# A fused retention and channel-mix kernel: a new hand order of all pieces, one block moved to full chunks, two scalings moved off GpSimd, and the last tile cut in three

## The chip, the core and the metric

The kernel runs on one core of a Trainium2 chip. The time is in device microseconds (us) of that core; a figure for a kernel is the median of its runs. The core has five engines that run side by side, each through its own list of instructions in order: TensorE (PE in the profile; its weight loads are PEld), VectorE (DVE), ScalarE (ACT), GpSimd (POOL) and SyncE (SP). An engine waits at an instruction until the semaphores that it names have been raised, and everything behind that instruction on the same engine waits too. Transfers between device memory and the on-chip memory (SBUF) are put in queues by SP, ACT and POOL. TensorE writes its products to PSUM, eight banks of 128 x 512 float32.

## The reference

The first part is a retention recurrence per head. The second is a channel mix with a shift by one token:

```python
# B=4, H=8, S=768, D=64; gamma[h] = 1 - 2**(-5-h); scale = 1/8
for t in range(S):
    state = gamma * state + outer(k[t], v[t])     # 64 x 64 per batch and head
    y[t] = scale * q[t] @ state
x = y, heads side by side                         # B x 768 x 512
xk = mu_k * x + (1 - mu_k) * x_prev               # x_prev: x one token earlier
xr = mu_r * x + (1 - mu_r) * x_prev
k = relu(xk @ w_k)                                # 512 -> 1024
v = (k * k) @ w_v                                 # 1024 -> 512
out = sigmoid(xr @ w_r) * v
```

Inputs and output are float32. The kernel computes the products in float16 with float32 sums, and turns the recurrence into products over chunks of tokens.

## The kernel before, in words

The 4 x 768 tokens are 12 **blocks** n = 0..11 of 256 tokens, three to a batch. All work is cut into **pieces**, and one text, `ORDER` (lines 24 to 75), lists them. The loop at line 745 reads it word by word and issues each piece. Since every engine runs its own pieces in this order, the text is the schedule; there is no other planner in the kernel. A word is a code, its arguments, after `~` an engine (v VectorE, a ScalarE, p GpSimd, s SyncE) and after `@` the PSUM banks. Counting an engine's words off along the timeline of the trace gives each instruction its piece, and the prediction names instructions so.

The pieces of a block n, with their engine and line:

- `lq`, `lk`, `lv`: loads of q, k and v (lines 232 and 237), nearly all from GpSimd's queue; a float32 source is written as float16 for q and k. v stays float32 and is multiplied by powers of gamma and cast in `vs` (line 255), on VectorE, for blocks 1 and 3 on GpSimd. `cq`, `ck` (line 245) are casts of the first half of block 0, which SP loads.
- `Tq`, `Tk`: TensorE transposes q and k (lines 274, 280); `Eq`, `Ek`: ScalarE copies them out of PSUM (line 243).
- `S`: scores k times q within a chunk (lines 320, 333, 341); `M`: VectorE copies them out under a causal mask (lines 349, 356).
- `C`: the block's part of the state, k times vs (lines 368, 386, 397); `U`: adds it to the carried state (line 421; for a batch's first chunk a copy, line 245 or 243); `G`: decays the state for the next block (line 426 on ScalarE, four instructions; the same function has a one-instruction form for VectorE).
- `I`, `J`: the product of q with the carried state (line 443); `Y`: masked scores times vs (lines 464, 480, 491). Both sum in one PSUM pair. `D`: VectorE scales it into x (lines 509, 516).
- `dx`: x minus x one token earlier (line 531). `X.n.w.j`: the mix for xk (w=0) or xr (w=1), columns j of four (line 560). Blocks 3 and 4, 6 and 7, 9 and 10 are mixed together (`GROUPS`).
- `K.n.g`: xk times w_k (lines 574, 584), after all four `X.n.0.j`; `Qa`, `Qb`: ScalarE's relu and square (lines 593, 601, 605). `R.n.tb`: xr times w_r (line 614), after all four `X.n.1.j`; `s`: sigmoid (line 620). `V.n.tb.half`: times w_v (line 626); `O`: VectorE's final product (line 632); `st`: the store (line 639).
- `z.c`: products of zeros on TensorE that nothing reads, c//4 of float32 and c%4 of float16 (lines 693, 700). `mu`, `mt`, `me`: load, transpose and copy of mu_k and mu_r (lines 676, 681, 684). `gy.0`, `gy.1`: a table of powers of gamma (lines 718, 711). `wk`, `wr`, `wv`: loads of the weights, on GpSimd's queue.
- `Vc`, `Oc`, `sc`: V, O and store of the very last 128 tokens by column parts (lines 644, 651, 659).

A block in `HALF` is worked in chunks of 64 tokens: 32 products of 64 x 64 for S, one mask instruction of 128 x 1024, three or four U, two instructions for D. A block in `WIDE` has chunks of 128 tokens: S in two parts with a mask instruction of 128 x 1024 each, one or two U, one D, and 16 products of 128 columns for Y. Before, blocks 2 to 4 are WIDE and 5 to 11 HALF.

```python
    def decayed(e, n):                       # G
        if e is nc.scalar:
            for j in range(NJ):
                nc.scalar.activation(...)
            return
        e.tensor_tensor(out=TG[0](n + 1), in0=T32(n), in1=gd[...], op=ALU.mult)
```

## Time and profile before

| | us |
|---|---|
| median of 3 runs (156.02 to 158.55) | 156.29 |
| the profiled execution | 156.68 |
| its span, first to last instruction | 154.9 |
| what lies around the span | 1.78 |
| TensorE busy | 146.0 |
| VectorE busy | 126.9 |
| ScalarE busy | 99.4 |
| GpSimd busy | 55.5 |
| bytes moved | 22.31 MB |

A record of a matmul holds its way through the array, so records overlap: four products of 512 columns are recorded with 379 ns each, but start 216 ns apart. What a piece costs TensorE is read from start to start. VectorE's records overlap by some 0.08 us when an instruction does not need the one before it, and stand 0.03 us apart when it does. The granted TensorE clock is 1.000 over the whole span.

### The profile page before, as it was taken

How to read it: one execution, taken by the hardware profiler on the slowest of the kernel's cores; microseconds unless marked ns; L12 is line 12 of the kernel's file. 1: busy time of each engine (PE TensorE's matmuls, PEld its weight loads, DVE VectorE, ACT ScalarE, POOL GpSimd, SP SyncE). 2: the span in 40 equal slices, each digit the busy share in tenths (PEclk: the TensorE clock that was granted, in tenths of full speed). 3: DMA queues.
4: the chain of work that ended last, by engine and by line, in shares of the span. 5: the costliest groups of instructions: out<-in, count | busy, mean ns of one | idle time of the engine just before them, and what ended most of it. 6: DMA issues, size and time to landing. Idle time of an engine off the chain costs nothing.

```text
span 154.9 us, 5520 instructions
## 1 busy us (share of the span) xinstructions
PE 146.0 (94%) x2423; PEld 83.9 (54%) x2423; DVE 126.9 (82%) x205; ACT 99.4 (64%) x186; POOL 55.5 (36%) x65
## 2 busy tenths in 40 slices
...
DMA packets 45768, 22.31 MB, mean 144 GB/s; under 512 B 37416, under 2 KB 41392, under 8 KB 45744
## 3 DMA queue, kind: packets, MB, share of 16 engines
...
q14 instruction: 5, 0.04, 0.1%
...
## 4 chain that ended last, share of the span: by engine, by line
PE 55%; DVE 24%; DMA 12%; issue 4%; POOL 3%; DVEq 0%; POOLq 0%
PE ps L626 19%; DMA v<-in_v_dram 12%; PE ps L614 9%; PE ps L574 9%; PE ps L584 8%; DVE a L356 3%; DVE xk L560 3%; DVE xr L560 3%; DVE vs L255 3%; DVE dx L531 2%; DVE xT L516 2%; DVE tg L421 2%; DVE os L632 2%; PE ps L443 2%; DVE a L349 1%
## 5 line engine op out<-in xcount | busy, mean ns | idle before, releaser
L626 PE MATMUL ps<-wv,k2s 128*128 128x512 f16 x184 | 43.4, 379 | 0.0
L593 ACT ACTIVATE kr<-ps 128x512 f32<-128x512 f32 x48 | 27.8, 596 | 23.1 <-PE ps L574 18.0
L626 PEld LDWEIGHTS <-k2s 128*128 128x128 f16 x184 | 17.4, 98 | 20.0
L632 DVE SCALAR_TENSOR_TENSOR os<-ps,rs 128x512 f32<-128x512 f32 x23 | 15.4, 683 | 14.5 <-ACT rs L620 7.4
L614 PE MATMUL ps<-wr,xr 128*128 128x512 f16 x96 | 24.1, 380 | 0.0
L584 PE MATMUL ps<-xk,wk 128*128 128x256 f16 x192 | 24.0, 273 | 0.0
L232 POOL DMA_DIRECT2D k<-in_k_dram x20 | 17.7, 898 | 15.2 <-PE ps L280 10.5
L574 PE MATMUL ps<-xk,wk 128*128 128x512 f16 x96 | 22.5, 379 | 0.0
L584 PEld LDWEIGHTS <-wk 128*128 128x128 f16 x192 | 18.1, 98 | 4.9 <-DMA wk<-in_moe_w_k_dram 0.6
L620 ACT ACTIVATE rs<-ps 128x512 f32<-128x512 f32 x24 | 13.7, 594 | 9.3 <-PE ps L614 8.9
L560 DVE SCALAR_TENSOR_TENSOR xr<-dx,mu,xT 128x256 f16<-128x256 f32 (+1 forms) x36 | 19.2, 564 | 0.1
L560 DVE SCALAR_TENSOR_TENSOR xk<-dx,mu,xT 128x256 f16<-128x256 f32 (+1 forms) x36 | 18.8, 567 | 0.2
L232 POOL DMA_DIRECT2D v<-in_v_dram x18 | 16.2, 915 | 1.4 <-DMA q<-in_q_dram 0.5
L243 ACT COPY kT<-ps 128x1024 f16<-128x1024 f16 (+1 forms) x13 | 12.2, 947 | 5.2 <-PE ps L280 4.1
L601 ACT ACTIVATE k2s<-kr 128x512 f16<-128x512 f32 x24 | 14.9, 628 | 0.3
L574 PEld LDWEIGHTS <-wk 128*128 128x128 f16 x96 | 9.2, 98 | 10.8
L531 DVE TENSOR_TENSOR dx<-xT 128x1024 f32<-128x1024 f32 x12 | 14.6, 1223 | 0.3
L605 ACT ACTIVATE k2s<-kr 128x512 f16<-128x512 f32 x24 | 14.5, 628 | 0.1
L243 ACT COPY qT<-ps 128x1024 f16<-128x1024 f16 (+1 forms) x13 | 12.3, 949 | 2.4 <-PE ps L274 2.2
L614 PEld LDWEIGHTS <-xr 128*128 128x128 f16 x96 | 8.8, 97 | 9.2 <-DVE xr L560 0.2
L255 DVE TENSOR_TENSOR vs<-v,csm_sb 128x1024 f16<-128x1024 f32 x10 | 12.1, 1216 | 2.0 <-DMA v<-in_v_dram 2.0
L356 DVE TENSOR_TENSOR a<-ps,c_sb 128x1024 f16<-128x1024 f32 (+1 forms) x12 | 12.2, 1040 | 0.5 <-PE ps L333 0.4
...
## 6 DMA issues: line engine op xcount, KB each, us to landing
...
wk<-in_moe_w_k_dram POOLq DMA_DIRECT2D x2, 512.0 KB, 11.0
...
```

The lines of the kernel that those rows point to most:

```text
L232: e.dma_start(out=dst[:, :, i * D : i * D + D], in_=src[:, i * P : i * P + P].rearrange("h p d -> p h d"),)
L243: e.copy(out=out, in_=in_)
L255: e.tensor_tensor(out=VS(n), in0=V32(n).rearrange("p h (i d) -> p i h d", i=2), in1=gks[:, int(half(n) or wide(n)), :, :, None].to_broadca ...
L356: nc.vector.tensor_tensor(out=a_full(n)[:, i, :, j0:j1], in0=pairs(banks("S", n, i, j0))[:, :, j0:j1], in1=(below if wide(n) else causal[: ...
L531: e.tensor_tensor(out=DX(k)[:, :, m * TM + t0 : m * TM + t1], in0=x[:, :, c + t0 : c + t1], in1=x[:, :, c - 1 + t0 : c - 1 + t1], op=ALU.s ...
L560: nc.vector.scalar_tensor_tensor(out=XM[w](k)[:, j, t0:t1], in0=DX(k)[:, j, t0:t1], scalar=mu[:, w * NCO + j : w * NCO + j + 1], in1=x[:, ...
L574: nc.tensor.matmul(banks("K", n, g), lhsT=wk16[:, co, g * P : g * P + P], rhs=XM[0](k)[:, co, :], start=(co == 0), stop=(co == NCO - 1),)
L584: nc.tensor.matmul(pz[:, i, :], lhsT=wk16[:, co, fo * P : fo * P + P], rhs=XM[0](k)[:, co, m * TM + t0 : m * TM + t1], start=(i == 0 and c ...
L593: nc.scalar.activation(out=kr, in_=banks("K", n, g, *u), func=AF.Relu)
L614: nc.tensor.matmul(banks("R", n, tb), lhsT=XM[1](k)[:, co, t : t + P], rhs=wr16[:, co, :], start=(co == 0), stop=(co == NCO - 1),)
L626: nc.tensor.matmul(banks("V", n, tb), lhsT=K2(n)[:, fo, tb * P : tb * P + P], rhs=wv16[:, fo, :], start=(fo == 0), stop=(fo == NFO - 1),)
L632: nc.vector.scalar_tensor_tensor(out=OS(2 * n + tb), in0=banks("V", n, tb), scalar=1.0 / (KSC * KSC), in1=RS(2 * n + tb), op0=ALU.mult, op ...
```

## The change

The words of `ORDER` are put in a new order. Beyond the order itself:

- Block 5 moves from HALF to WIDE: `S.5`, `M.5` become two parts each, `U.5.1` and `U.5.2` go, `J.5` comes.
- `vs.1` and `vs.3` move from GpSimd to VectorE. No computation is left on GpSimd, which then only queues transfers.
- `gy.1` moves from ScalarE to VectorE, `cq` from VectorE to ScalarE; `U.0.0`, `U.3.0` and `U.9.0` from VectorE to ScalarE; `G.7` and `G.9` from ScalarE to VectorE.
- The zero products are dealt out anew; the first word `z.12` becomes four words `z.3`. `mt` moves ahead of the first transposes.
- On the queues, `lk.0.0.2` now stands ahead of `lq.0.0.2` on SP, `lq.0.2.4` ahead of `lv.0` on GpSimd, `wk.1` behind `lv.2` and `lk.2`, both `wv` together; `lv.7` instead of `lv.11` is queued by SP.
- The last 128 tokens are cut into columns 0 to 255, 256 to 383 and 384 to 511 (`CUTS`) instead of two halves.

The diff, cut to the stretches that the prediction speaks of:

```diff
 KUP = 4.0
-HALF = (5, 6, 7, 8, 9, 10, 11)
+HALF = (6, 7, 8, 9, 10, 11)
...
-WIDE = (2, 3, 4)
+WIDE = (2, 3, 4, 5)
 HEADS = ((0, 1), (3, 2), (4, 5), (7, 6))
+CUTS = ((0, 256), (256, 384), (384, 512))
 ORDER = """
-lq.0.0.2~s gy.0 lv.0~p lk.0.0.2~s ck.0.0.2~v mu lk.0.2.4~p lq.0.2.4~p gy.1~a lv.1~p lk.1~p lq.1~p
-cq.0.0.2~v lq.2~p wk.0~p z.12@6 Tk.0.0.2@0 Tq.0.0.2@1 Ek.0.0.2~a Eq.0.0.2~a mt@2 wk.1~p vs.0~v
-z.2@6 S.0.0.0.2@01 me M.0.0.0.2~v S.0.1.0.2@45 Tk.0.2.4@2 M.0.1.0.2~v Tq.0.2.4@3 lk.2~p C.0@67
-U.0.0~v Ek.0.2.4~a Eq.0.2.4~a z.1@0 S.0.0.2.4@23 M.0.0.2.4~v I.0@45 S.0.1.2.4@01 M.0.1.2.4~v z.1@2
-Y.0 U.0.1 G.0~a vs.1~p Tk.1@7 Ek.1~a D.0~v dx.0~v lv.2~p lq.3~p lk.3~p C.1@01 U.1.0 X.0.0.0
-X.0.0.3 Tq.1@6 Eq.1~a z.4@2 S.1.1@67 lq.4~p X.0.0.2 I.1@45 Tq.2@0 M.1.1~v S.1.0@23 Eq.2~a wr~p
-X.0.0.1 z.1@7 K.0.0@6 M.1.0~v U.1.1 G.1~a lk.4~p Qa.0.0 X.0.1.0 X.0.1.1 Qb.0.0 Y.1 D.1~v dx.1~v
-X.1.0.1 z.1@3 K.0.3@7 X.1.0.2 Qa.0.3 K.0.2@1 X.1.0.0 Qa.0.2 X.1.0.3 Tk.2@6 K.0.1@0 Ek.2~a vs.2~v
-S.2.0@67 S.2.1@45 M.2.0~v Qb.0.3 K.1.1@1 K.1.2@2 Qa.0.1 Qb.0.2 lv.3~p C.2@0 Qa.1.2 Tq.3@3 Eq.3~a
-U.2.0 I.2@67 Tk.3@0 Qa.1.1 K.1.0@2 Tq.4@1 X.1.1.0 Ek.3~a Qa.1.0 M.2.1~v Y.2 lq.5~p Eq.4~a S.3.0@45
...
-R.1.1@7 X.2.0.1 vs.3~p M.3.0~v Ek.4~a K.2.3@1 Qa.2.3 K.2.0@6 Qa.2.0 M.3.1~v S.4.1@45 M.4.1~v
-Tq.5@1 Eq.5~a C.3@23 U.3.0~v U.3.1 s.1.1 vs.4~v R.1.0@6 s.1.0 G.3~a K.2.1@0 I.3@45 Qb.2.3 S.4.0@23
...
-lv.5~p vs.5~v K.3.5@0 Qa.3.5 Qa.3.3 K.3.4@6 V.1.1.1 Qa.3.2 lv.6~p C.5@01 S.5@45 Qa.3.4 vs.6~v
-C.6@23 Qb.3.3 Qb.3.2 O.1.1 M.5~v U.5.0 X.2.1.3 U.5.1 U.6.0~a U.6.1 U.6.2 U.5.2 U.6.3 K.3.0@6
...
-Qb.5.1 V.4.0.1 X.6.0.1 lq.9~p G.7~a V.3.0.0@3 V.3.1.1 V.3.0.1 U.8.0 K.6.3@4 Qa.6.3 O.4.0 K.6.1@5
...
-G.9~a vs.11~v U.10.0 U.10.1 U.10.2 Qb.6.5 M.10~v st.5.1 R.6.0@1 s.6.0 R.7.0@0 s.7.0 K.8.1@1 Qa.8.1
...
-Qb.11.1 X.11.1.1 O.8.0 K.11.3@1 s.9.1 V.9.1.0@3 V.10.1.0@0 s.8.1 O.8.1 st.8.1 R.11.1@6 V.9.0.0@7
-Qa.11.3 V.11.0.0@1 s.10.0 Qa.11.2 Qb.11.2 R.10.1@2 V.9.1.1 O.9.1 V.10.1.1 s.10.1 O.10.1 st.9.1
-Qb.11.3 V.9.0.1 st.10.1 s.11.1 Vc.11.1.1@2 s.9.0 V.10.0.0@6 O.9.0 R.11.0@0 V.11.0.1 st.8.0 st.9.0
-s.11.0 Oc.11.1.1 sc.11.1.1~a O.11.0 st.11.0 V.10.0.1 O.10.0 st.10.0 Vc.11.1.0@0 Oc.11.1.0
-sc.11.1.0~s
+lk.0.0.2~s lq.0.2.4~p lq.0.0.2~s lv.0~p mu z.3@6 z.3@6 z.3@6 z.3@6 mt@0 cq.0.0.2~a ck.0.0.2~v
+Tk.0.0.2@1 Ek.0.0.2~a Tq.0.0.2@2 Eq.0.0.2~a me z.4@6 S.0.0.0.2@23 gy.0 gy.1~v Tq.0.2.4@1
+Eq.0.2.4~a vs.0~v S.0.1.0.2@45 lk.0.2.4~p Tk.0.2.4@0 Ek.0.2.4~a C.0@67 M.0.0.0.2~v U.0.0~a
+M.0.1.0.2~v S.0.0.2.4@01 M.0.0.2.4~v lv.1~p I.0@23 S.0.1.2.4@45 U.0.1 M.0.1.2.4~v z.3@0 Y.0 vs.1~v
+G.0~a D.0~v dx.0~v X.0.0.1 X.0.0.0 lk.1~p Tk.1@4 Ek.1~a lq.1~p z.3@0 Tq.1@5 Eq.1~a z.4@3 S.1.1@45
+lq.2~p Tq.2@2 Eq.2~a C.1@67 X.0.0.3 X.0.0.2 U.1.0 z.2@3 I.1@01 M.1.1~v S.1.0@23 M.1.0~v wk.0~p
+K.0.1@6 Qa.0.1 K.0.0@4 Qa.0.0 X.0.1.3 U.1.1 lv.2~p vs.2~v Qb.0.1 Y.1 D.1~v dx.1~v lk.2~p z.5@2
+C.2@4 Tk.2@5 G.1~a U.2.0 z.1@2 I.2@01 wk.1~p K.0.3@4 X.1.0.3 Ek.2~a S.2.0@67 Qa.0.3 S.2.1@23
+Qb.0.3 X.1.0.1 X.1.0.0 X.1.0.2 K.1.1@5 K.0.2@4 Qa.1.1 Qb.1.1 lk.3~p K.1.0@5 X.0.1.2 Qa.0.2 X.0.1.0
...
+K.2.0@5 s.0.1 Qb.0.2 Qa.2.0 K.2.2@1 vs.3~v C.3@67 U.3.0~a Qa.2.2 M.3.0~v lk.5~p Tk.5@0 Ek.5~a
+S.4.0@45 lv.4~p S.4.1@23 U.3.1 I.3@67 G.3~a K.2.1@1 K.1.3@0 M.4.0~v vs.4~v Qa.2.1 Qb.2.1 Y.3
...
+D.3~v dx.3~v Y.4 K.2.3@5 S.5.0@67 M.5.0~v J.4 X.2.1.0 D.4~v dx.4~v s.1.1 wv.0~p Tk.6@01 Qa.2.3
...
+K.3.7@1 vs.5~v Qa.3.7 O.0.0 O.0.1 Qb.3.3 lv.6~p st.1.1 S.5.1@23 vs.6~v S.6@67 M.6~v Tq.7@45 Eq.7~a
+C.5@0 R.2.0@1 U.5.0 lv.7~s C.6@67 U.6.0~a I.5@45 K.3.2@0 s.2.0 Qa.3.2 Qb.3.2 M.5.1~v Y.5 U.6.1
+U.6.2 U.6.3 S.7@23 M.7~v I.6@01 J.5 K.3.6@6 vs.7~v G.6~a K.3.5@7 K.3.4@2 D.5~v dx.5~v X.5.0.1
...
+lq.10~p X.6.0.2 vs.8~v K.5.0@1 X.5.1.2 X.5.1.3 G.7~v Qa.5.0 Qb.5.0 lv.10~p V.4.0.1 O.3.0 st.2.0
...
+S.9@01 Tq.10@67 M.9~v Y.8 D.8~v dx.8~v X.8.0.2 X.8.0.3 V.5.1.0@4 K.6.4@0 G.9~v R.6.0@1 R.5.0@2
...
+O.9.1 V.10.0.0@3 st.9.1 s.10.0 Vc.11.1.1@5 V.10.1.1 R.11.1@6 O.9.0 s.10.1 O.10.1 st.9.0 V.11.0.0@7
+V.10.0.1 O.10.0 st.10.1 s.11.1 st.10.0 R.11.0@6 s.11.0 Oc.11.1.1 sc.11.1.1~a V.11.0.1 O.11.0
+Vc.11.1.0@2 st.11.0 Oc.11.1.0 sc.11.1.0~s Vc.11.1.2@6 Oc.11.1.2 sc.11.1.2~a
 """
...
     def values_c(e, n, tb, c):
-        x = slice(c * dm // 2, (c + 1) * dm // 2)
+        x = slice(*CUTS[c])
...
     def result_c(e, n, tb, c):
-        x = slice(c * dm // 2, (c + 1) * dm // 2)
+        x = slice(*CUTS[c])
...
     def store_c(e, n, tb, c):
-        x = slice(c * dm // 2, (c + 1) * dm // 2)
+        x = slice(*CUTS[c])
```

More of the change, by code (lines that the diff above doesn't have):

```diff
@@ new lines @@
+S.9@01 Tq.10@67 M.9~v Y.8 D.8~v dx.8~v X.8.0.2 X.8.0.3 V.5.1.0@4 K.6.4@0 G.9~v R.6.0@1 R.5.0@2
+X.8.0.1 Eq.10~a s.6.0 V.5.1.1 O.5.1 s.5.0 C.10@67 U.10.0 U.10.1 I.9@23 Qa.6.4 Qb.6.2 Tq.11@01
+Qb.6.4 Eq.11~a V.5.0.1 U.10.2 R.6.1@4 s.6.1 U.10.3 Qb.6.6 S.10@01 G.10~a I.10@67 Y.9 X.8.0.0
+M.10~v K.8.3@4 st.3.0 K.8.0@0 Qa.8.3 D.9~v Qa.8.0 R.7.1@1 vs.11~v s.7.1 K.8.2@4 C.11@23 Qa.8.2
+Qb.8.0 Qb.6.7 Tk.11@01 O.5.0 st.5.0 st.5.1 U.11.0 U.11.1 U.11.2 Y.10 D.10~v Ek.11~a V.7.0.0@5
+V.6.0.0@4 I.11@23 S.11@01 M.11~v X.8.1.1 X.8.1.2 dx.9~v dx.10~v X.9.0.0 X.9.0.3 X.9.0.2 V.7.0.1
```

54 lines of the change are left out of this document (25 added, 29 removed).

## The prediction

> **What bounds the kernel now.** I read the busy times first, then the chain of waits, then the groups by shape, then the timeline, whose instructions I named by counting off the words of ORDER. On the page:
>
> ```profile
> PE 146.0 (94%) x2423; PEld 83.9 (54%) x2423; DVE 126.9 (82%) x205; ACT 99.4 (64%) x186; POOL 55.5 (36%) x65
> ```
>
> Two engines are nearly full (its first part: busy time, share of the span), so the question is which one ends last where. The chain of waits in order of time (start, length, what) answers it:
>
> ```profile
> 8.16 0.45 DVE vs L255
> ...
> 74.64 0.43 DVE tg L421
> 75.08 0.04 issue
> 75.12 0.29 PE ps L443 x12
> ...
> 150.42 0.89 PE ps L644 x8
> 151.31 0.02 issue
> 151.33 0.42 DVE os L651
> ```
>
> Mostly VectorE sets the pace until 75 us; from then TensorE runs to 151.3 almost without a gap. Busy time in stretches of the span shows the same (the stretch, its length, then busy us and instructions of PE, PEld, DVE, ACT and POOL; granted clock, DMA share, GB/s):
>
> ```profile
> 16.00:20.00 4.00, 2.91 (x75) 2.21 (x79) 4.00 (x8) 1.01 (x1) 1.33 (x2) 1.00 1.56 191
> 130.00:140.00 10.00, 10.00 (x64) 6.06 (x63) 2.42 (x5) 9.03 (x18) 0.00 (x0) 1.00 0.07 26
> ```
>
> At 16 to 20 us VectorE is full and TensorE is not; at 130 to 140 it is the reverse. VectorE's last mix (X.11.1.1) ends at 131.03. So the end is: the time at which VectorE lets TensorE into its dense run, plus all TensorE work behind that point, plus what TensorE still waits. A change of order must be judged by this sum. I take it at K.1.1, the first point of dense running that both orders pass with almost the same pieces done. From the timeline (start, length, engine, what):
>
> ```profile
> 7.58 0.20 PE L681 MATMUL ps<-csm_sb,mu 8*128 8x8 f32 x1 [0.84 <-DMA mu<-in_moe_mu_r_dram]
> ...
> 24.23 0.62 PE L333 MATMUL ps<-qT,kT 64*128 64x128 f16 x16
> 24.79 1.95 PE L584 MATMUL ps<-xk,wk 128*128 128x256 f16 x16
> ...
> 38.92 0.44 PE L386 MATMUL ps<-vs,k 128*64 128x64 f16 x16 [0.52 <-POOL vs L255]
> ```
>
> The second line is S.2, the third begins with K.1.1: it starts at 24.79, and TensorE ends 151.29 - 24.79 = 126.5 later.
>
> **The change: VectorE's own work.** The groups by shape (count, busy time, mean ns of one, idle time before):
>
> ```profile
> L255 DVE TENSOR_TENSOR vs<-v,csm_sb 128x1024 f16<-128x1024 f32 x10 | 12.1, 1216 | 2.0 <-DMA v<-in_v_dram 2.0
> L255 POOL TENSOR_TENSOR vs<-v,csm_sb 128x1024 f16<-128x1024 f32 x2 | 3.8, 1918 | 3.7 <-DMA v<-in_v_dram 3.6
> L421 DVE TENSOR_TENSOR tg<-ps,tg 128x256 f16<-128x256 f32 x22 | 9.0, 417 | 0.4
> L356 DVE TENSOR_TENSOR a<-ps,c_sb 128x1024 f16<-128x1024 f32 x8 | 9.7, 1218 | 0.5 <-PE ps L333 0.4
> ```
>
> Two scalings come to VectorE: 2 x 1.22 = 2.43. G.7 and G.9 are not shown there; nearest is U at 0.42 (bounds 0.29 and 0.68, VectorE's rows of half and twice the size): 0.84. gy.1 (128 x 512) lies between 0.42 (128 x 256, L718) and 1.22: the 128 x 512 mask takes 0.68, I take 0.69. cq leaves: -0.41. Three first copies U leave: 3 x -0.42 = -1.25. Block 5 wide: two U less (-0.84), one mask more (+1.22), one D of 1.23 for two of 0.69 (-0.15): +0.23. A third Oc: +0.16, as two of 128 columns at about 0.29 (L718, 128 x 128) stand for one of 0.42. Sum: +2.7, so VectorE goes from 126.9 to 129.6.
>
> GpSimd's scalings might have cost VectorE more than they show. They ran at 10.97 to 12.91 and 36.97 to 38.88. VectorE's masks and U beside them took 0.69, 0.42 and 1.22, their usual times, so I give nothing back.
>
> **The start.** mt now stands ahead of the first transposes, and mu_r's transfer ended it at 7.58 in this profile; Tk, before at 6.11, comes at about 7.65. Ek and Eq (0.59 each) then end at 9.2, z.4 beside them costs two records at 0.53, and S of block 0 follows by 9.6. v now is second in GpSimd's queue, behind a half load of q. It landed at 8.14 before; the halves behind it landed 0.4 and 1.2 later, so I take 8.6. k, now first on SP, lands near 4.0 as q did, so ck, gy.0 (2.05) and gy.1 (0.69) run ahead, 4.0 to 7.5, in a wait. vs.0 starts at 8.65, not 8.16, and covers the late transposes; without that cover (mu later than 7.7) every 0.1 goes straight into the sum.
>
> From vs.0 VectorE now does, until the end of U.2.0, at start-to-start rates read from the timeline (vs 1.14, M 1.13 and 0.61 for a half, U 0.34, D 1.26, dx 1.25, X 0.40): 3 vs 3.42; 4 half M 2.44; 2 M 2.26; 4 U 1.36; 2 D 2.52; 2 dx 2.50; 5 X 2.00. Together 16.5. The second k half is queued third and lands at about 9.3, as the third did; its transpose, copy and scores end at 11.5 and hold up the third mask by 0.5. So U.2.0 ends at 25.7. TensorE stands there: I.2 (0.3) waits for U.2.0, and K.0.3 (0.87), S.2 (0.66) and K.1.1 are queued behind I.2. K.1.1 starts at 27.6: **2.8 later than before**. The new zero products (twelve at first, then z.3, z.3, z.4, z.2, z.5, z.1) all lie ahead of this point, beside VectorE's work, and cost nothing as long as that is longer.
>
> **Behind K.1.1.** Of the pieces done ahead of it, K.0.2 is now behind (+0.87), C.2 and I.2 are ahead (-0.45). Block 5 wide: S 0.66 as S.4 for 0.38 as S.6; C 0.15 for 0.19; I, J and Y 1.0 for 0.56 in all (as block 4 against block 5): +0.65. The last tile's two pieces of 128 columns replace one of 256, 8 x 0.109 = 0.87. A product of this form is not shown. It costs no less than the columns, half of 0.109, and no more than 0.109; the transposes of 128 columns (0.6 for 16, two side by side) put it near 0.065, so +0.2 (bounds 0 and 0.87). The Trainium skill, "TensorE: Matmul & The Clock Gate", section "Back-to-back issue gap", gives 81 ns for 128 columns with weight loads, which would make it +0.43; it gives 131 ns for 512 columns too, where this trace has 216, so I stay with the rows. Sum: 126.5 + 0.87 - 0.45 + 0.65 + 0.2 = 127.8.
>
> In these 126.5 TensorE waits some 2.0 in six gaps, by the starts: 0.49 before I.2, 0.68 before C.3, and four of 0.15 to 0.25. C.3's goes: it waited for GpSimd's vs.3, which began when v landed (36.83) and took 1.9. VectorE reaches vs.3 at about 38 and needs 1.22. I take 0.8 off. What is late next: VectorE's words from vs.0 to the last mask of block 5 sum to 52.6 at these rates, so with 0.6 of waits it is there at 61.9, and TensorE at Y.5 at 62.8. A margin of 0.9 is why I take off no more.
>
> **The sum.** TensorE ends at 27.6 + 127.8 - 0.8 = 154.6 (before 151.3). Before, 3.6 followed to the end of the span; a last Oc of 128 columns saves 0.1: 3.5. Span 158.1. With 1.78 around it: 159.9 against the profiled 156.68. The median lies 0.39 under that execution, so the median comes to 159.5.
>
> **Rivals.** *The front runs without the waits that I put in.* v lands no later than before, the third mask doesn't wait, VectorE starts at 8.16: K.1.1 at 26.6, and the gaps behind shrink to 1.2, as in the forecast. Then 158.5. For it: VectorE has work to fill a wait, such as vs.1 between Y.0 and D.0, where it stood 0.52. Against: its work up to U.2.0 is fixed.
>
> *The front slips further.* mt at the head of TensorE, or loads behind a changed queue. mu_r's last packet started at 6.72 behind packets of k and v; if it lands 1 us later, transposes, S and all masks follow. Or TensorE's waits stay 2.0 and bank reuse adds as much as before. Each alone gives 160.5 to 161; both 162.
>
> *Not slower: TensorE's pieces shrink.* Taken each at its shortest start-to-start time in this trace (K, R and V 0.86, S of a half block 0.27, Tq 0.26, C 0.19, Y 0.41), the pieces in the 126.5 come to 117. The 9.5 above that are the 2.0 of gaps and a stretch of pieces around a change of shape: a K of 0.87 takes 0.97 behind 64-column products, Tq 0.41. If the new order groups like pieces and finds every result ready, so that half of it goes (4.7), TensorE ends at 150.7 and the median is 155.6. It decides from 4 us upward, where the 2.8 of the front and the 1.3 of added work are paid. Against: TensorE can get only 0.9 ahead before it stands at VectorE, by the count at Y.5.
>
> *GpSimd's scalings held VectorE.* If VectorE stood for both (3.84), that time comes back and the median is 155.7. No VectorE instruction beside them is longer than usual, and its longest stand there (0.52 ahead of D.0) ends with TensorE. The Trainium skill, "SBUF — State Buffer", section "Who interferes with whom", says that a VectorE instruction with two SBUF inputs and a GpSimd instruction that reads SBUF shut each other out for the whole instruction. This trace has no such pair: every VectorE instruction beside the scalings had an input in PSUM.
>
> **Chances.** Forecast 0.52 (159 to 161); front without waits 0.25; front slips 0.19; pieces that shrink 0.03; scalings that held VectorE 0.01. A measurement of this kernel can tell about 2% from no change: 159.4 and 153.2 are the bounds. The forecast lies on the upper one; 0.38 of its 0.52 is above, with the slip 0.57. The rest up to 1 is within 2%, but for 0.02 faster. The range leaves out the last two and the far end of the slip: 157.4 to 161.8.
>
> **What would show it.** Right: K.1.1 at 27 to 28 us, TensorE waiting for U.2.0 just ahead; VectorE busy 129 to 130; no wait of C.3 for vs.3; TensorE's last product near 154.6. Wrong: K.1.1 at 25 or earlier, a TensorE run behind it shorter than 126, or VectorE idle for several us because TensorE or a load is late.

## The result and the profile after

The changed kernel takes **156.81 us** (median of 20 runs, 156.14 to 158.35), the kernel before 156.45 in the same comparison (20 runs, 155.58 to 159.44). The ratio is 1.0038, with a 95% interval from 1.002 to 1.0056: 0.2 to 0.6% slower, where 2% was forecast. A repetition gave 156.54 against 156.18 (ratio 1.0016, 0.9991 to 1.0042, which includes no change). The ratio leaves out the four executions of the kernel before that took 158.3 us and more, and "at full clock" below means the median of the executions with a mean granted clock of 0.995 or more (the last section shows what happens in others), set beside the same median of the kernel before in that run's comparison, 156.0 to 156.5. The changed kernel has 156.57 at full clock, and 156.54 in the repetition.

The profiled execution took 156.27 us, its span is 154.5. Its busy times, and then the shares by engine in the chain of waits, from the profile's page:

```profile
PE 147.5 (95%) x2381; PEld 84.6 (55%) x2381; DVE 129.5 (84%) x205; ACT 98.8 (64%) x178; POOL 51.8 (34%) x63
```

```profile
PE 84%; DVE 6%; DMA 4%; issue 3%; ACT 1%; POOL 1%; POOLq 0%; DVEq 0%
```

VectorE's work came out as forecast (129.6). But the chain now lies on TensorE for 84% of the span. The same line of the kernel before has 55% there, with 24% on VectorE and 12% on transfers:

```profile
PE 55%; DVE 24%; DMA 12%; issue 4%; POOL 3%; DVEq 0%; POOLq 0%
```

Busy time in stretches of the changed kernel (stretch, length, then busy us and instructions of PE, PEld, DVE, ACT, POOL; then the granted clock, the DMA share and GB/s):

```profile
16.00:20.00 4.00, 3.92 (x106) 2.87 (x97) 3.93 (x8) 1.61 (x2) 2.18 (x3) 1.00 1.61 214
26.44:151.08 124.64, 124.64 (x1988) 71.69 (x1984) 107.63 (x163) 85.75 (x154) 32.40 (x37) 1.00 0.79 132
130.00:140.00 10.00, 10.00 (x63) 5.98 (x62) 3.81 (x8) 7.33 (x15) 0.00 (x0) 1.00 0.27 99
```

The second row is the prediction's "behind K.1.1": TensorE is busy in all of its 124.64 us. The same row of the kernel before, from its K.1.1 to its last product, has 1.1 us of idle time between its records:

```profile
24.79:151.29 126.50, 125.39 (x2052) 71.24 (x2048) 107.61 (x165) 85.48 (x158) 36.06 (x40) 1.00 0.81 131
```

So the later entry (26.44 instead of 24.79) is given back by a run that is 1.9 us shorter, although work was added to it. The entry in the timeline of TensorE after: the stand for U.2.0, which the prediction named, and, behind K.0.3 and S.2, K.1.1 as the first piece of the last row:

```profile
24.67 0.31 PE L444 MATMUL ps<-qT,tg 64*64 64x128 f16 x8 [1.01 <-DVE tg L422]
...
26.44 2.79 PE L585 MATMUL ps<-xk,wk 128*128 128x256 f16 x24
```

The scalings, from the groups: twelve at the same 1.22 us, and the wait for v that was 2.0 us in all is 0.6.

```profile
L256 DVE TENSOR_TENSOR vs<-v,csm_sb 128x1024 f16<-128x1024 f32 x12 | 14.6, 1221 | 0.6 <-DMA v<-in_v_dram 0.6
```

By kind of piece, from start to start behind K.1.1, the time that went is: q's transposes 4.78 to 3.49 (the stands before I.2 and C.3 came behind Tq.3 and Tq.5, which took 0.94 and 1.16, now 0.54 and 0.47), C 2.95 to 2.55, I 1.99 to 1.62, S 4.02 to 3.76 with one more part. K grew by 0.31, with one more in the stretch, and V by 0.28.

### The profile page after: what moved, and what is told of

Its sections match the earlier page's. It is cut to its first block, busy times and chain, and to the rows that moved or that the text cites. A ratio compares the mean times of both kernels' runs of the same rounds, so it can differ in the third digit from the quotient of the medians.

```text
span 154.5 us, 5438 instructions
## 1 busy us (share of the span) xinstructions
PE 147.5 (95%) x2381; PEld 84.6 (55%) x2381; DVE 129.5 (84%) x205; ACT 98.8 (64%) x178; POOL 51.8 (34%) x63
## 4 chain that ended last, share of the span: by engine, by line
PE 84%; DVE 6%; DMA 4%; issue 3%; ACT 1%; POOL 1%; POOLq 0%; DVEq 0%
PE ps L627 26%; PE ps L615 14%; PE ps L575 14%; PE ps L585 13%; DMA v<-in_v_dram 4%; PE ps L275 3%; PE ps L444 3%; PE ps L281 2%; DVE a L357 2%; PE ps L334 1%; PE ps L321 1%; PE ps L481 1%; PE ps L369 1%; PE ps L465 1%; PE ps L645 1%
## 5 line engine op out<-in xcount | busy, mean ns | idle before, releaser
L627 PE MATMUL ps<-wv,k2s 128*128 128x512 f16 x184 | 44.6, 380 | 0.0
L585 PE MATMUL ps<-xk,wk 128*128 128x256 f16 x192 | 23.5, 273 | 0.0
L233 POOL DMA_DIRECT2D v<-in_v_dram x18 | 16.1, 918 | 6.0 <-DVE xr L561 1.7
L256 DVE TENSOR_TENSOR vs<-v,csm_sb 128x1024 f16<-128x1024 f32 x12 | 14.6, 1221 | 0.6 <-DMA v<-in_v_dram 0.6
L357 DVE TENSOR_TENSOR a<-ps,c_sb 128x1024 f16<-128x1024 f32 (+1 forms) x14 | 14.6, 1066 | 0.0
```

What stands on the lines that cost most here:

```text
L233: e.dma_start(out=dst[:, :, i * D : i * D + D], in_=src[:, i * P : i * P + P].rearrange("h p d -> p h d"),)
L256: e.tensor_tensor(out=VS(n), in0=V32(n).rearrange("p h (i d) -> p i h d", i=2), in1=gks[:, int(half(n) or wide(n)), :, :, None].to_broadca ...
L357: nc.vector.tensor_tensor(out=a_full(n)[:, i, :, j0:j1], in0=pairs(banks("S", n, i, j0))[:, :, j0:j1], in1=(below if wide(n) else causal[: ...
L585: nc.tensor.matmul(pz[:, i, :], lhsT=wk16[:, co, fo * P : fo * P + P], rhs=XM[0](k)[:, co, m * TM + t0 : m * TM + t1], start=(i == 0 and c ...
L627: nc.tensor.matmul(banks("V", n, tb), lhsT=K2(n)[:, fo, tb * P : tb * P + P], rhs=wv16[:, fo, :], start=(fo == 0), stop=(fo == NFO - 1),)
```

## The experiments

The edits show the words around a change; the rest of a line is left out. "Theory" and "rival" are those of the text ahead of each result.

**Repetition** (a_again). The changed kernel, unchanged.

> The changed kernel once more, to stand beside the next runs on the same chip. If the small difference to the kernel before is real: ratio 1.002 to 1.006, K.1.1 near 26.4, TensorE 124 to 125 us from K.1.1 to its end, mu landed before the zero products end (no wait at mt). If mt's early place can go wrong: the transposes of block 0 start after 6.5 in this profile and the front is later by as much.

156.54, ratio 1.0016 (0.9991 to 1.0042), as given above. Its profiled execution is one with a stretch of half clock (last section): K.1.1 comes at 28.33, and TensorE's run behind it is 124.65 us, the same as in the first profile.

**vs.1 back on GpSimd, at its word** (a_vs1p). The words ahead of it stay.

```diff
-M.0.1.0.2~v S.0.0.2.4@01 M.0.0.2.4~v lv.1~p I.0@23 S.0.1.2.4@45 U.0.1 M.0.1.2.4~v z.3@0 Y.0 vs.1~v
+M.0.1.0.2~v S.0.0.2.4@01 M.0.0.2.4~v lv.1~p I.0@23 S.0.1.2.4@45 U.0.1 M.0.1.2.4~v z.3@0 Y.0 vs.1~p
```

> The changed kernel with vs.1 back on GpSimd. Theory A: VectorE sets the start of K.1.1 and its work there counts one to one. Then K.1.1 comes 1.1 earlier (near 25.3), TensorE stays dense behind it, and the time is 1.0 to 1.2 shorter than the changed kernel's: ratio to the kernel before 0.995 to 0.998. Rival B: TensorE's list or its waits behind set the time whatever the front does; K.1.1 comes earlier, but the waits behind it grow and the ratio stays at 1.002 to 1.006.

162.49, ratio 1.0391 (1.0365 to 1.0418). GpSimd's timeline: it waits 5.77 us for v, then scales, and only then can issue k of block 1; TensorE's shows what that does:

```profile
10.46 1.90 POOL L256 TENSOR_TENSOR vs<-v,csm_sb 128x1024 f16<-128x1024 f32 x1 [5.77 <-DMA v<-in_v_dram]
12.31 0.93 POOL L238 DMA_DIRECT2D k<-in_k_dram  x1
...
16.86 1.06 PE L275 MATMUL ps<-c_sb,k 128*64 128x128 f16 x16 [3.76 <-DMA k<-in_k_dram]
```

A computing instruction in the queue that issues the loads costs what stands behind it. Part of the 6 us is the clock: the granted clock is 0.50 from 16 to 20 us, behind TensorE's stand. This run priced the queue, not the scaling, so I repeated it with the loads ahead.

**vs.1 on GpSimd, behind the loads up to lk.2** (a_vs1p2). The loads are taken from their later places.

```diff
-z.3@0 Y.0 vs.1~v
+z.3@0 Y.0 lk.1~p lq.1~p lq.2~p wk.0~p lv.2~p lk.2~p vs.1~p
```

> The changed kernel with vs.1 on GpSimd behind the loads up to the second k of block 2, so that no load waits for it (in the first try it stood ahead of them). Theory A: VectorE sets the start of K.1.1 one to one and TensorE stays dense behind it: K.1.1 at 25.2 to 25.5 in a profile without a slow clock stretch, 1.0 to 1.2 shorter than the change, ratio to the kernel before 0.994 to 0.997. Rival B: VectorE's later work and waits take the lead back: ratio 1.000 to 1.004.

156.51, ratio 1.0018 (0.9993 to 1.0042): no gain from 1.14 us less on VectorE. VectorE's timeline says where it went:

```profile
13.14 1.22 DVE L517 TENSOR_TENSOR xT<-ps,gy_sb 128x1024 f32<-128x1024 f32 x1 [0.85 <-PE ps L444]
...
17.59 0.42 DVE L422 TENSOR_TENSOR tg<-ps,tg 128x256 f16<-128x256 f32 x1 [0.26 <-PE ps L398]
...
24.45 0.42 DVE L422 TENSOR_TENSOR tg<-ps,tg 128x256 f16<-128x256 f32 x1
```

It stands 0.85 before D.0 and 0.26 before U.1.0, together 1.11, and U.2.0 (the last row) starts 16.1 after vs.0 (8.34), as in the changed kernel (24.20 - 8.09). There vs.1 fills those waits.

**vs.1 twice, vs.9 twice** (a_vs1x2, a_vs9x2). Is there any slack left, in front or further on? The second scaling writes the same values again.

```diff
-z.3@0 Y.0 vs.1~v
+z.3@0 Y.0 vs.1~v vs.1~v
```

> The changed kernel with the scaling vs.1 of block 1 done twice on VectorE, between Y.0 and D.0. With vs.1 taken off VectorE the end of U.2.0 stayed where it was, because VectorE then stood 0.85 before D.0 and 0.26 before U.1.0. Theory A (the order was filled exactly: VectorE waits for nothing there with vs.1 in place): a second scaling of 1.14 goes through in full: K.1.1 at 27.4 to 27.7, 1.0 to 1.2 us slower, near 157.6. Theory B (TensorE's chain of small products sets the time of the front and VectorE still has slack in it): K.1.1 within 0.4 of 26.44, 0 to 0.4 slower.

157.37 at full clock, 1.1 above the kernel before; 0.7 above the changed kernel by the comparisons, and by the traces 1.1 (K.1.1 27.53, span 155.6). TensorE's stand before I.2 grows from 1.01 to 1.50:

```profile
25.76 0.31 PE L444 MATMUL ps<-qT,tg 64*64 64x128 f16 x8 [1.50 <-DVE tg L422]
```

The same with vs.9, in the middle of the dense run:

> The changed kernel with the scaling of block 9 done twice on VectorE (1.14 more work at 88 us, the result is the same). The profile of the change shows VectorE just in time there (X.8.0.0 ends at 104.80, K.8.3 starts at 105.11). If VectorE still paces TensorE this late: 0.7 to 1.1 slower than the change. If TensorE alone paces the second half, with VectorE's waits taking it up: 0 to 0.3.

157.55, ratio 1.008 (1.0061 to 1.0099). TensorE stands 0.86 where the changed kernel has no gap:

```profile
89.76 0.69 PE L369 MATMUL ps<-vs,k 64*64 64x64 f16 x56 [0.86 <-DVE vs L256]
```

So VectorE's time is filled without slack: one more scaling costs 0.7 to 1.1 us of its 1.14 to 1.22, at 13 us as at 88. That one less gives nothing is shown at 13 us alone.

**Parts of the change in the old order.** First the two scalings on VectorE (b_vs13v):

```diff
-Y.0 U.0.1 G.0~a vs.1~p Tk.1@7
+Y.0 U.0.1 G.0~a vs.1~v Tk.1@7
...
-R.1.1@7 X.2.0.1 vs.3~p M.3.0~v
+R.1.1@7 X.2.0.1 vs.3~v M.3.0~v
```

> The kernel before, in its old order, with vs.1 and vs.3 on VectorE instead of GpSimd; nothing else. By the step of the prediction (added VectorE work ahead of the dense run counts in full) K.1.1 is 1.1 later and the waits around vs.3, some 0.8, go: 0.8 to 1.6 slower, ratio 1.005 to 1.010. If VectorE's extra work is hidden in waits it has anyway: ratio 0.998 to 1.002.

157.27, ratio 1.0062 (1.0038 to 1.0086): 1.0 us slower. In its profiled execution (0.6 longer than that of the kernel before) K.1.1 comes 0.5 later, at 25.28, and the run behind it is as long as before, 126.6. Then block 5 in chunks of 128 tokens (b_wide5):

```diff
-HALF = (5, 6, 7, 8, 9, 10, 11)
+HALF = (6, 7, 8, 9, 10, 11)
...
-WIDE = (2, 3, 4)
+WIDE = (2, 3, 4, 5)
-lv.6~p C.5@01 S.5@45 Qa.3.4 vs.6~v
-C.6@23 Qb.3.3 Qb.3.2 O.1.1 M.5~v U.5.0 X.2.1.3 U.5.1 U.6.0~a U.6.1 U.6.2 U.5.2 U.6.3
+lv.6~p C.5@0 S.5.0@45 Qa.3.4 vs.6~v
+C.6@23 Qb.3.3 Qb.3.2 O.1.1 M.5.0~v S.5.1@45 M.5.1~v U.5.0 X.2.1.3 U.6.0~a U.6.1 U.6.2 U.6.3
...
-Y.5 X.3.1.0
+Y.5 J.5 X.3.1.0
```

> The kernel before with block 5 alone in chunks of 128 tokens (two S and two M for one, one U for three, J added), the second S behind the first mask in the same banks. By the prediction's term: TensorE 0.65 more, VectorE 0.23 more, so 0.5 to 0.9 slower: ratio 1.003 to 1.006. Rival: one TensorE wait for the second S or mask adds to it, up to 1.5; or the work hides and the ratio is 0.998 to 1.002.

158.72, ratio 1.0158 (1.0123 to 1.0193): 2.4 us slower, where the prediction priced the part at 0.65 of TensorE and 0.23 of VectorE. TensorE's timeline holds the reason for half of it, a stand before S.5.1 that comes from where I put it (it must wait until M.5.0 has emptied its banks); the other half was not split up:

```profile
60.02 0.40 PE L333 MATMUL ps<-qT,kT 64*128 64x128 f16 x8 [1.29 <-DVE a L356]
```

And the three-part tail (b_tail3), whose `slice` line changes in all three functions:

```diff
+CUTS = ((0, 256), (256, 384), (384, 512))
...
-        x = slice(c * dm // 2, (c + 1) * dm // 2)
+        x = slice(*CUTS[c])
...
-sc.11.1.0~s
+sc.11.1.0~s Vc.11.1.2@6 Oc.11.1.2 sc.11.1.2~a
```

> The kernel before with one part of the change alone: its last 128 tokens in three column pieces (256, 128, 128). The prediction took 0.2 us more on TensorE (8 products of 128 columns at 0.065 each in place of half of 0.87) and 0.1 less behind its last product: 0.1 slower. The trace of the changed kernel has these 8 products in 0.45 us, twice that in 0.89, against 0.87 for one piece of 256: 0.02 more on TensorE, and a last product on VectorE of 0.29 instead of 0.42: 0.1 faster. Both are at the edge of what a comparison can tell; the trace tells more: the end of the last Oc, 151.75 in the kernel before, is at 151.65 by the one and at 151.85 by the other, if TensorE starts the last tile at the same time.

156.30, ratio 1.0 (0.998 to 1.0019): nothing that this can tell. The eight products of 128 columns take 0.45 us in its trace and in the changed kernel's, half of the 0.87 to 0.89 for 256 columns, so the part costs TensorE 0.02 and not the forecast 0.2.

So two of the parts cost 1.0 and 2.4 when put into the old order, against some 0.4 for the whole change. The rest of the change, the new order above all, takes the difference back; which words of it do so was not tried.

**Does the late start close the gaps?** TensorE enters the dense run 1.65 us later than before. Zero products ahead of K.1.1 of the old order do the same to it (b_z7):

```diff
-S.2.0@67 S.2.1@45 M.2.0~v Qb.0.3 K.1.1@1 K.1.2@2
+S.2.0@67 S.2.1@45 M.2.0~v Qb.0.3 z.7@1 K.1.1@1 K.1.2@2
```

> The kernel before with one word of zero products (z.7, 1.7 us of TensorE by z.4's 1.06 and z.3's 0.65) put ahead of K.1.1, so that TensorE enters the dense run 1.7 us later than it could, as it does in the changed kernel (26.44 against 24.79). Theory A (the gaps behind K.1.1 belong to the old order): they stay or move, and the end comes 1.2 to 1.7 us later: near 157.7. Theory B (they vanish because TensorE enters later, so that VectorE and the loads are ahead): the gaps before I.2 (0.49), C.3 (0.68) and the four smaller ones are filled, some 1.5 to 2.0 in all, and the end comes 0 to 0.3 later; the changed kernel then owes its dense run to its late start and not to its placing of the pieces. In between, the share of the 1.7 that is swallowed is the share of the gaps that the late start explains.

159.13, ratio 1.0194 (1.0171 to 1.0218), 3.0 us slower at full clock. Neither theory allows that. The timelines of VectorE, GpSimd and TensorE show what came in between:

```profile
35.74 3.34 DVE L560 SCALAR_TENSOR_TENSOR xk<-dx,mu,xT 128x256 f16<-128x256 f32 x4
...
36.12 1.90 POOL L255 TENSOR_TENSOR vs<-v,csm_sb 128x1024 f16<-128x1024 f32 x1 [2.07 <-DMA v<-in_v_dram]
...
38.35 0.28 PE L584 MATMUL ps<-xk,wk 128*128 128x256 f16 x1 [0.67 <-DVE xk L560]
39.14 1.80 PE L584 MATMUL ps<-xk,wk 128*128 128x256 f16 x15 [0.50 <-DVE xk L560]
```

Four mixes take 3.34 us instead of 1.67: the second, X.2.0.0, runs from 36.15 to 38.30, 2.15 instead of 0.48, while GpSimd scales vs.3 (36.12 to 38.02). It reads two tiles in SBUF, as the scaling does. In the kernel before, vs.3 ran at 36.97, when VectorE was at masks with an input in PSUM. To ask the first question without this, the same word in b_vs13v, with both scalings on VectorE (b_vs13v_z7):

> The kernel before with both scalings on VectorE (run b_vs13v: 157.27, K.1.1 at 25.28, TensorE's end at 151.86, 0.33 of standing before I.2, 0.31 before S.4.1, 0.16 before C.3, 0.13 before C.6) and with the word z.7 (1.7 us of TensorE) ahead of K.1.1. No computation is on GpSimd, so that nothing can hold VectorE there. Theory A (the gaps belong to the old order, and the delay passes through): 1.4 to 1.8 above b_vs13v, 158.7 to 159.1. Theory B (a late start swallows the gaps): the four named stands vanish, some 0.9, and the smaller losses with them, and the time is 0 to 0.9 above b_vs13v: 157.3 to 158.2.

158.86, ratio 1.016 (1.0122 to 1.0198); at full clock 158.77, 1.5 above b_vs13v (1.2 if each is measured against its own kernel before), and its span is 157.2 against 155.5. Most of the delay passes through: K.1.1 comes 1.97 later than in b_vs13v (27.25 against 25.28), and the run behind it is 0.26 shorter (126.32 against 126.58). Of the named stands, only I.2's shrinks (0.33 to 0.14); S.4.1 still stands 0.31, C.3 0.17, C.6 0.12. With GpSimd's vs.3 in place a late start can close more: in b_tail3's trace, also of the old order, K.1.1 comes at 25.64, 0.85 later than in the profile of before, C.3 no longer waits for vs.3, and the run is 0.7 shorter (125.81). So a late start closes a part of the old order's gaps, 0.3 us with the scalings where the changed kernel has them; it doesn't explain a run that is 1.9 shorter.

**GpSimd beside VectorE** (a_vs11p2x). vs.11 twice on GpSimd behind Y.8, where GpSimd is idle:

```diff
-S.9@01 Tq.10@67 M.9~v Y.8 D.8~v dx.8~v
+S.9@01 Tq.10@67 M.9~v Y.8 vs.11~p vs.11~p D.8~v dx.8~v
...
-D.9~v Qa.8.0 R.7.1@1 vs.11~v s.7.1
+D.9~v Qa.8.0 R.7.1@1 s.7.1
```

> The changed kernel with vs.11 taken off VectorE and done twice on GpSimd, behind Y.8, where GpSimd has nothing else to do: from about 97.1 to 100.9. VectorE has D.8 there (97.5 to 99.0, its input in PSUM) and then dx.8 and X.8 (two SBUF inputs each). Theory A (a GpSimd instruction that reads SBUF and a VectorE instruction with two SBUF inputs shut each other out): D.8 takes its 1.48, and dx.8, the first X.8 or the second scaling is longer by 0.5 to 1.9 us; VectorE, which has no lead at K.8.3, hands that on, less what it regains where vs.11 is gone (which is behind K.8.3): 0.5 to 1.9 slower. Theory B (they run side by side): all rows as in the changed kernel (dx 1.22, X 0.48, scaling 1.92), the time the same within 0.3 us.

157.83, ratio 1.0091 (1.0055 to 1.0127). The timelines of GpSimd, VectorE and TensorE:

```profile
96.77 3.88 POOL L256 TENSOR_TENSOR vs<-v,csm_sb 128x1024 f16<-128x1024 f32 x2 [20.70 <-PE ps L465]
...
97.28 1.48 DVE L510 TENSOR_TENSOR xT<-ps,gy_sb 128x512 f32<-128x512 f32 x2
98.79 2.94 DVE L532 TENSOR_TENSOR dx<-xT 128x1024 f32<-128x1024 f32 x1
...
104.03 1.02 PE L615 MATMUL ps<-wr,xr 128*128 128x512 f16 x4 [1.05 <-DVE os L633]
```

D.8 (one input in PSUM) takes its usual 1.48 beside the first scaling. dx.8 (both in SBUF) takes 2.94 instead of 1.22: it ends 1.1 us after the second scaling, nearly as if it had started only when that was done. TensorE pays with a stand of 1.05. Theory A holds.

**vs.3 alone back on GpSimd, behind the loads up to lk.6** (a_vs3p2). The loads are taken from their later places.

```diff
-Qa.2.0 K.2.2@1 vs.3~v C.3@67
+Qa.2.0 K.2.2@1 lk.5~p lv.4~p lq.5~p lk.6~p vs.3~p C.3@67
```

> The changed kernel with vs.3 alone on GpSimd, behind lk.6 in its queue (in a_vs13p2 with vs.1 as well: 157.06 and 157.41 in its runs at full clock). It runs from about 35.8 to 37.7, beside masks and U of block 3 (one input in PSUM). Theory A (VectorE has no lead at block 5, so that the 1.14 us which it is spared counts, unless C.3, which waits for vs.3, is late): U.3 and the masks behind it 0.5 to 1.1 earlier, but TensorE has no gap to close there, so the time is the same within 0.3. Theory B (GpSimd's 1.92 makes C.3 late, as in the kernel before, where it waited 0.52): C.3 at 38.1 or later instead of 37.85, TensorE stands 0.3 to 0.6, and the time is 0.3 to 0.7 above the changed kernel's.

157.34, ratio 1.0022 (0.999 to 1.0054); 156.85 at full clock, 0.4 above the kernel before, as the changed kernel is. By the time that is theory A, by the profiled execution neither: C.3 did not wait. The mix X.2.0.3 did. By the timelines of VectorE, GpSimd and TensorE four mixes take 3.80 us, the last of them 2.60 (34.99 to 37.59), beside the scaling:

```profile
33.80 3.80 DVE L561 SCALAR_TENSOR_TENSOR xk<-dx,mu,xT 128x256 f16<-128x256 f32 x4
...
35.36 1.94 POOL L256 TENSOR_TENSOR vs<-v,csm_sb 128x1024 f16<-128x1024 f32 x1
...
37.65 1.58 PE L585 MATMUL ps<-xk,wk 128*128 128x256 f16 x13 [1.00 <-DVE xk L561]
```

This mix would have ended at 35.47, so 0.11 us of overlap cost 2.12. The six executions at full clock lie between 156.09 and 157.46, and the profiled one is the longest of them; whether the others escape the overlap is not known, as none of them was profiled. With both scalings on GpSimd (a_vs13p2, the two edits together):

> As the run with vs.1 on GpSimd behind the loads, and vs.3 on GpSimd too, behind four more loads. Theory A: behind K.1.1 TensorE is already dense, so 1.1 less on VectorE there gives 0 to 0.3 beyond the run with vs.1 alone: ratio 0.992 to 0.997. Rival: as in the kernel before, C.3 waits for GpSimd (0.5 or more) and the queue stands: 0.5 to 1.0 slower than with vs.1 alone.

158.89 over seven executions, ratio 1.0097 (1.0059 to 1.0136); two of them at full clock took 157.06 and 157.41. Its profiled execution took 292.95 us: TensorE's pieces last twice as long (K.1.1 1.68 from start to start instead of 0.88) although the granted clock on record is 1.00, so its trace tells nothing of the scalings.

**The zero products** (a_nozero). All but the first twelve are left out:

```diff
-Eq.0.0.2~a me z.4@6 S.0.0.0.2@23
+Eq.0.0.2~a me S.0.0.0.2@23
...
-M.0.1.2.4~v z.3@0 Y.0
+M.0.1.2.4~v Y.0
...
-lq.1~p z.3@0 Tq.1@5 Eq.1~a z.4@3 S.1.1@45
+lq.1~p Tq.1@5 Eq.1~a S.1.1@45
...
-U.1.0 z.2@3 I.1@01
+U.1.0 I.1@01
...
-lk.2~p z.5@2 C.2@4 Tk.2@5 G.1~a U.2.0 z.1@2 I.2@01
+lk.2~p C.2@4 Tk.2@5 G.1~a U.2.0 I.2@01
```

> The changed kernel without the seven later words of zero products (z.4, z.3, z.3, z.4, z.2, z.5, z.1, together some 6.4 us of TensorE's time between 6.6 and 23.7); only the first four words z.3 stay. Theory A (they lie in TensorE's waits for VectorE and cost nothing): U.2.0 and K.1.1 within 0.2 of 24.20 and 26.44, the same time within 0.3 us as long as the granted clock stays at 1.00; what they are worth is then seen in the clock alone: if TensorE's clock falls to half for the 3.4 us that it does in some executions of the changed kernel, the time is 1.0 to 1.3 more. Theory B (they hold real products up by some tenths): K.1.1 0.3 to 0.6 earlier and the time lower by as much.

161.06 (four runs, 157.92 to 162.24; mean granted clock 0.936 to 0.975). Stretches of its profile, as above:

```profile
12.00:16.00 4.00, 3.13 (x68) 2.84 (x68) 3.72 (x4) 2.13 (x6) 1.91 (x3) 0.50 1.50 202
16.00:20.00 4.00, 2.84 (x88) 2.34 (x87) 2.87 (x7) 1.53 (x2) 2.09 (x3) 0.50 1.62 218
20.00:24.00 4.00, 4.00 (x44) 2.58 (x36) 3.44 (x5) 0.81 (x2) 2.77 (x4) 0.51 1.72 185
```

The granted clock is 0.50, where the changed kernel has 1.00. K.1.1 comes at 30.61, 4.2 later. Since the clock changed with them, this run can't say what the zero products cost. In the changed kernel's trace they cost nothing in front, as forecast: VectorE, which sets the pace there, stands nowhere longer than 0.07 between vs.0 and U.2.0, and TensorE stands 1.01 behind the last of them. And they hold the clock: all four executions without them have a low one, and their median is 4.5 us above the changed kernel's at full clock, more than either part costs in the old order. Their kind at the start, twelve of float16 or z.12 as before, matters less (a_z12):

```diff
-mu z.3@6 z.3@6 z.3@6 z.3@6 mt@0
+mu z.12@6 mt@0
```

> The changed kernel with its first twelve float16 zero products put back to three float32 ones, as before the change. Theory C: the first zero products decide in which runs the clock is granted late, and the median of the change (0.4% above before, although its profiled span is shorter) comes from runs with a clock of 0.985 to 0.99. Then the clocks are 1.0 in nearly all runs and the ratio is 0.998 to 1.001. Rival: the clock has nothing to do with them; ratio 1.002 to 1.006 as for the change.

156.69, ratio 1.0019 (0.9998 to 1.0039): the same as the changed kernel. One of its 12 executions has a low mean clock (0.985), against 7 of 32 of the changed kernel: too few to tell whether the kind matters for the clock.

**What sets the front: v, mu or k** (a_vfirst, a_vfirst2). v of block 0 queued ahead of the half of q:

```diff
-lk.0.0.2~s lq.0.2.4~p lq.0.0.2~s lv.0~p mu
+lk.0.0.2~s lv.0~p lq.0.0.2~s lq.0.2.4~p mu
...
-gy.0 gy.1~v Tq.0.2.4@1 Eq.0.2.4~a vs.0~v S.0.1.0.2@45
+gy.0 gy.1~v vs.0~v S.0.1.0.2@45 Tq.0.2.4@1 Eq.0.2.4~a
```

> The changed kernel with the load of v for block 0 ahead of the half load of q on GpSimd's queue, and the transposes and copy of that half of q behind the scores S.0.1.0.2. In the changed kernel VectorE stands 0.61 us before vs.0, until v lands at 8.06; the table gy.1 is done at 7.47. Theory (the time is the point at which VectorE lets TensorE into its dense run, plus a dense run without gaps): v lands some 0.6 earlier, vs.0 starts at 7.5 to 7.7, the masks follow, U.2.0 and K.1.1 come 0.3 to 0.5 earlier (K.1.1 at 26.0 instead of 26.44), and all of that is kept to the end: 0.3 to 0.5 below the changed kernel, at or just below the kernel before. Rival 1: the third mask then waits for the second half of k, which lands no earlier, and K.1.1 stays within 0.15 of 26.44: no difference. Rival 2: the front comes earlier but VectorE or a load is late at block 5 or behind, and the gain is lost there: K.1.1 at 26.0 and an end within 0.15 of 151.08.

157.05, ratio 1.0066 (1.0037 to 1.0094): 0.3 to 0.4 slower than the changed kernel. vs.0 starts at 7.29, even earlier than the theory had it, but (timelines of TensorE and VectorE)

```profile
7.03 0.21 PE L682 MATMUL ps<-csm_sb,mu 8*128 8x8 f32 x1 [0.67 <-DMA mu<-in_moe_mu_r_dram]
...
9.22 1.29 DVE L357 TENSOR_TENSOR a<-ps,c_sb 128x512 f16<-128x512 f32 x2 [0.70 <-PE ps L342]
11.16 0.69 DVE L357 TENSOR_TENSOR a<-ps,c_sb 128x512 f16<-128x512 f32 x1 [0.65 <-PE ps L342]
```

mu lands at 7.03 and holds the transposes behind it, the first mask waits 0.70 and the third 0.65, and K.1.1 comes at 27.18. The first is the prediction's late mu with no late v to cover it, the second its wait at the third mask, for which it took 0.5. With mu's transpose moved behind the first scores as well:

```diff
-z.3@6 mt@0 cq.0.0.2~a ck.0.0.2~v
+z.3@6 cq.0.0.2~a ck.0.0.2~v
...
-Eq.0.0.2~a me z.4@6 S.0.0.0.2@23 gy.0
+Eq.0.0.2~a z.4@6 S.0.0.0.2@23 mt@0 me gy.0
```

> As a_vfirst (v of block 0 loaded ahead of the half of q), but with the transpose of mu behind the first scores and not ahead of the first transposes. In a_vfirst mu landed at 7.03 and the transposes with it at 7.18, S at 8.80, VectorE stood 0.70 before its first mask and 0.65 before its third, and K.1.1 came at 27.18: 0.74 later instead of 0.4 earlier. Theory A (mu ahead of the transposes was the whole of that): the transposes run at 6.4, S at 8.0 to 8.3, vs.0 at 7.3 to 7.5 is followed at once by the masks; the third then waits some 0.3 for the second half of k; K.1.1 at 25.9 to 26.2 and the time 0.3 to 0.5 below the changed kernel's, 156.0 to 156.3. Theory B (the loads land in the sum no earlier, whatever their order: the second half of k or the first of q comes late in v's place): K.1.1 at 26.3 to 27, no gain or a loss up to 0.5.

156.86, ratio 1.0062 (1.0036 to 1.0088). Theory B: the first mask no longer waits, but v landed only at 7.93, and the second half of k holds the third mask:

```profile
7.93 1.23 DVE L256 TENSOR_TENSOR vs<-v,csm_sb 128x1024 f16<-128x1024 f32 x1 [0.62 <-DMA v<-in_v_dram]
9.07 1.28 DVE L357 TENSOR_TENSOR a<-ps,c_sb 128x512 f16<-128x512 f32 x2
10.98 0.69 DVE L357 TENSOR_TENSOR a<-ps,c_sb 128x512 f16<-128x512 f32 x1 [0.63 <-PE ps L342]
```

v was queued at the same place in both, and had landed by 7.29 in the one and at 7.93 in the other: the place in the queue alone does not fix a landing. Nor did K.1.1 come earlier than the changed kernel's 26.44 in either (27.18 and 27.00).

**TensorE's stand before I.2** (a_i2). I.2 moved behind S.2, X.0.1.3 behind X.1.0.2:

```diff
-Qa.0.0 X.0.1.3 U.1.1 lv.2~p
+Qa.0.0 U.1.1 lv.2~p
...
-U.2.0 z.1@2 I.2@01 wk.1~p K.0.3@4 X.1.0.3 Ek.2~a S.2.0@67 Qa.0.3 S.2.1@23
+U.2.0 z.1@2 wk.1~p K.0.3@4 X.1.0.3 Ek.2~a S.2.0@67 Qa.0.3 S.2.1@23 I.2@01
...
-X.1.0.2 K.1.1@5
+X.1.0.2 X.0.1.3 K.1.1@5
```

> The changed kernel with I.2 moved behind K.0.3 and S.2 on TensorE, so that nothing stands behind U.2.0, and with the mix X.0.1.3 (0.40 us of VectorE, needed by R.0.0 only) moved behind X.1.0.2. In the changed kernel TensorE stands 1.01 us before I.2 until U.2.0 ends at 24.62; K.1.1 starts at 26.44, and its inputs X.1.0 are ready at 26.20, by this order at 25.8. Theory A (the sum: point of entry plus the work behind it): K.1.1 at 25.8 to 26.0, and all of it is kept: 0.4 to 0.6 below the changed kernel, 156.0, level with the kernel before or better. Theory B (VectorE, with no lead at blocks 3 to 5, sets the pace until then): K.1.1 at 25.8 to 26.0, but TensorE stands 0.4 to 0.6 more in all before Y.2, C.3 (which waits for vs.3), or Y.5, and the end is within 0.15 us of the changed kernel's.

156.36, ratio 0.9998 (0.9966 to 1.003): level with the kernel before. At full clock it is 156.34, 0.2 to 0.4 below the changed kernel, less than theory A and more than B, but the intervals of the two kernels overlap (0.9966 to 1.003 and 0.9991 to 1.0042), so no gain is shown. The edit missed its aim: K.0.3 writes bank 4, which holds C.2 until U.2.0 has read it, so TensorE's stand moved to it:

```profile
25.82 1.03 PE L585 MATMUL ps<-xk,wk 128*128 128x256 f16 x8 [1.10 <-DVE tg L422]
```

(The times of this trace lie about 1 us later, after a stretch at half clock.) What is left of the edit is the mix of 0.40 us out of the way of U.2.0. Whether the stand itself could be had stays open.

## Why the prediction was wrong

The sum was made as entry plus run, and both terms were too long: the profiled end of TensorE came at 151.1, not 154.6, and the median at 156.8, not 159.5. The median misses by less (2.7 us) than the profiled execution (156.27 against 159.9, 3.6), because that execution happens to lie 0.54 below the median. "Within 2%" had a chance of 0.41, slower 0.57, and the low end of the range was 157.4.

- **VectorE's own work**: 129.6 forecast, 129.5 measured. Right.
- **The front's work**: 16.5 us of VectorE from vs.0 to the end of U.2.0 at start-to-start rates; 16.53 measured (8.09 to 24.62). TensorE stood there for U.2.0, as said (1.01). Right, and a_vs1x2 shows that more of it passes through.
- **The front's waits**: 0.5 for v and 0.5 at the third mask were put in; in the changed kernel's profile neither came (vs.0 at 8.09, the third mask at 10.43 right behind the second). K.1.1 was at 26.44, not 27.6: 1.16 of the miss. This was the rival "front without waits" (0.25), whose 26.6 for K.1.1 was right; its 158.5 was not, since it kept the gaps. Such waits exist (a_vfirst has 0.70 and 0.65), but I carried landings from one profile of the old order of loads into the new one, and added two waits that take each other's place. In eleven traces of the new order of loads mt runs between 5.80 and 6.64, and not at 7.58; vs.0 starts between 7.76 and 8.66, so 8.65 was the late end of it; and the third mask waits in only three of them, 0.22 to 0.40, all with vs.0 before 8.0. Where v is late, the scores are there in time.
- **Behind K.1.1, the constant**: this is the step that failed most. I carried TensorE's 126.5 over as a sum of work, took off 0.8 of 2.0 us of gaps (by the starts; the records, which overlap, leave 1.1 idle), and added 1.3. Measured: 124.6, so 2.4 of the miss. The gaps are gone altogether (1.2 more than I took off), the tail cost 0.02 instead of 0.2, and the remaining 1.0 is the balance of pieces around a change of shape, some of them shorter (C.10 0.61 before and 0.28 after, Tk.7 0.61 and 0.37, Y.6 0.57 and 0.35), some longer (C.8 0.19 and 0.35). One part was a plain slip: I.2 moved ahead of K.1.1, and I left its gap of 0.49 in the run behind. The rival "pieces shrink" pointed the right way with 0.03, but needed half of 9.5 us; about 3 came. That this length belongs to the order is borne out by nine traces with the new order behind K.1.1 and a clock of 1.00 there: they enter between 26.44 and 32.77 (a_vs1p), and the run is 124.5 to 124.8 us in all of them. No trace enters earlier than 26.2, so whether the run would stay free of gaps from the old kernel's 24.79 on is not shown.
- **The reason for keeping the gaps**: TensorE could get only 0.9 us ahead at Y.5 before it would stand at VectorE. Measured, Y.5 starts 0.13 after M.5.1 ends, K.5.1 0.03 after X.5.0.3, K.8.3 0.31 after X.8.0.0. A small margin was no sign of waits: at these places each result is ready just in time.
- **C.3 and vs.3**: no wait, as forecast (vs.3 ends at 37.67, C.3 starts at 37.85).
- **The rival that GpSimd's scalings held VectorE** (0.01): the trace of before gave it no ground, as said, since no such pair of instructions was in it. The Trainium skill, "SBUF — State Buffer", section "Who interferes with whom", has the two shut each other out for the whole instruction; b_z7, a_vs3p2 and a_vs11p2x show it, at 1.7, 2.1 and 1.7 us a time, and the PSUM instruction beside them unharmed, as the section says too. In the new order the move to VectorE thus ends a risk, and no gain in time is shown for it: at a place without such a neighbour (a_vs1p2) the same scaling on GpSimd costs nothing.

Part by part, then: in the old order the scalings cost 1.0 and the wide block up to 2.4; in the new order VectorE waits less (its waits of more than 0.05 us behind vs.0 and up to 126 us sum to 3.7 before and 1.6 after) and TensorE's gaps are closed, and all but 0.3 to 0.6 is given back. How much of this each move of a word is worth was not tried.
